# Two layers of attention and MLP, forward and backward: w2's products of layer 1 spread over its backward pass, and the last turns of w1 set behind the first products

## The chip, the cores and the metric

The kernel runs on one core of one Trainium2 chip. Its time is the device time of one execution in microseconds (us); the median of three runs of the kernel before is 1107.51 us (1107.36 to 1107.98). A core has TensorE (PE; its weight loads are shown apart as PEld), VectorE (DVE), ScalarE (ACT), GpSimd (POOL) and SyncE (SP), which run their own instruction lists and wait for one another by semaphores, and 16 DMA engines that move data between the chip's memory (DRAM) and the on-chip memory SBUF. PE writes into the banks of PSUM.

## What is computed

Two layers, each an attention block that reads a cache and an MLP, for two sequences of one token, and then the gradients of everything against a given `grad_out`:

```python
def _A_ref(x, k_cache, v_cache, wq, wo):      # Hq = 32, Hkv = 4, Sk = 16384, Dh = 128
    q = (x @ wq).reshape(B, Sq, Hq, Dh).transpose(0, 2, 1, 3)
    k = jnp.repeat(k_cache, rep, axis=1)
    v = jnp.repeat(v_cache, rep, axis=1)
    p = _softmax(jnp.einsum("bhqd,bhkd->bhqk", q, k) * (Dh ** -0.5))
    o = jnp.einsum("bhqk,bhkd->bhqd", p, v)
    return o.transpose(0, 2, 1, 3).reshape(B, Sq, Hq * Dh) @ wo

def _B_ref(x, w1, b1, w2, b2):                # D = 1024, F = 3584
    h = _gelu(jnp.einsum("bsd,df->bsf", _layernorm(x), w1) + b1)
    return jnp.einsum("bsf,fd->bsd", h, w2) + b2

x = A_x
x = x + _A_ref(_layernorm(x), k_cache, v_cache, wq, wo)
x = x + _B_ref(_layernorm(x), w1, b1, w2, b2)
x = x + _A_ref(_layernorm(x), k_cache, v_cache, wq, wo)
x = x + _B_ref(_layernorm(x), w1, b1, w2, b2)
```

`out_0` is x at the end; `out_1` to `out_9` are the gradients of x, of the K and V caches, and of the weights and biases. Both layers share the caches and the weights, so each of the four passes (forward of layers 0 and 1, backward of layers 1 and 0) reads the caches and the attention weights, and each MLP, forward and back, the MLP weights. The page counts 348.15 MB read and 98.62 MB written. Everything is bfloat16 in DRAM.

## The kernel before

**A list of pieces, planned before it is written out.** The function does not issue instructions as it goes. `emit(fn, uses)` appends a piece of work and the memory chunks that it uses to a list, and `Program.run` goes through the list at the end, calls each piece, and so writes the instructions of all engines in the order of the list. Within an engine this is the order of execution.

**Chunks and slots.** A chunk is up to 1 MB of a cache or a weight (`ld_kv`, `ld_rows`, `ld_w2`, ...), or a place without a load (a turned copy, a row to store). A slot is 128 partitions x 4096 bf16, 1 MB. There are 16 slots of their own, and parts of other tiles serve as slots while those tiles are not in use; their names (`ds`, `e`, `late`) stand in the profile. Before layer 0's backward pass some slots end as places of loads and become staging for stores (`HALF_AT`, `FULL_AT`); nine serve loads to the end, one of which the chunk `Y` keeps. `run` asks, ahead of every piece, whether the next load can have a free slot, where next means in the order of the pieces that first use the chunks. It gives the slot if all chunks in between still find room (`possible`), and writes the load's `dma_start` to SP's queue at that place. A chunk gives its slot back after its last piece. SP's queue is in order: a load whose slot is still read, or still being stored from, holds up the loads behind it. `keep` leaves a chunk in its slot between two passes where there is room all the way, so that its second load falls away.

**The backward pass of attention**, `attn_bwd`, runs in steps, `s = 0, 1, ...`. In layer 1's pass, step s turns a piece of a V chunk on DVE (`kblock`, L537) and multiplies it on PE two blocks later (L550); 14 steps behind it (`LAG_B`) a piece of a K chunk is multiplied (`direct`, L575). A V chunk and a K chunk last four steps each. wo's and wq's tiles are turned by PE and ACT (`turn_here`, L452 and L455) and multiplied (`here_products`, L465) in the steps between. There are 128 steps of V and 14 more. The caller hands in `extra`, a table from a step to pieces that are put at that step's end; at the end of the pass they come in the same order.

**What layer 1's `extra` holds.** `w2_fwd_piece(1, ws2b, i, fps1)` is the MLP's second product in the forward direction for w2's tile i of seven: 32 matmuls (L877) into `fps1`. After the seventh, `x_out` adds bias and residual (L1441), and `col_to_row` makes the row of `out_0` of it: two transposes on PE (L616), a copy on DVE (L617) into a chunk of kind `"load"`, that is into a slot of loads, and a store on POOL's queue (L618). The same seven tiles are used once more: each of their 28 pieces is turned in place (`w2_turns`, L452 and L455), and the turned ones are multiplied with layer 0's gradient after the pass (L1526 to L1530), so every tile keeps its slot from its first product to the end.

**The joint between the passes** (L1520 to L1599). After layer 1's pass come its layer norm, w2's products, `dh0_` (L1532, with `spread_h0`, L506 and L507), and the products of w1: `t1` holds sixteen turns on DVE (L437), two for each of eight chunks of w1, and `p1` eight groups of 28 matmuls (L487), one for each chunk. Between the groups stand the first units of w1's and w2's gradients: rows turned and copied (L1289, L1309, L268), outer products (L1326) cast by ACT (L276) and stored by POOL (L1356). Then the layer norm's backward and layer 0's attention pass follow, whose outputs fill PE, DVE and ACT.

Of the kernel before, what the change touches and what calls it, by code (L numbers as in the profile page):

```python
# [57 lines left out]
class Program:  # L58
# [12 lines left out]
    def emit(self, fn, uses=()):  # L71
        i = len(self.ops)
        self.ops.append((fn, tuple(uses)))
        for c in uses:
            if c.first is None:
                c.first = i
            c.last = i
# [105 lines left out]
def kernel(  # L183
# [46 lines left out]
    emit = P.emit  # L230
# [23 lines left out]
    def ob():  # L254
        st["ob"] += 1
        return obanks[st["ob"] % len(obanks)]


    def load_of(engine, us):
        st[engine] += us  # L260
        m = min(st["act"], st["dve"])
        st["act"] = min(st["act"] - m, 6.0)
        st["dve"] = min(st["dve"] - m, 6.0)
# [127 lines left out]
    def ld_w2():  # L391
        return [ld_rows("w2", B_w2, 4 * i, 4, 0, D) for i in range(FJ // 4)]

    def col(c, j, n, o):
        return c.ap[:, j * n + o * 128:j * n + (o + 1) * 128]
# [213 lines left out]
    def col_to_row(colT, dram_out, queue=None, kind="half"):  # L609
        c = P.chunk(kind=kind)  # L610

        def f():
            row = c.ap[0:DJ, 0:256].rearrange("p (b n) -> p b n", b=2)
            ps = ob()[0:DJ, 0:256].rearrange("p (b n) -> p b n", b=2)
            for b in range(2):
                PE.transpose(ps[:, b, :], colT[:, :, b], identf[:])  # L616
            V.tensor_copy(out=row, in_=ps)  # L617
            (queue or GP).dma_start(dram_out.rearrange("b (j n) -> j b n", n=128), row)  # L618

        return f, [c]  # L620
# [252 lines left out]
    def w2_fwd_piece(l, ws, i, fps):  # L873
        def f():
            for j in range(4):
                for o in range(DJ):
                    PE.matmul(fps[:, o, :], lhsT=col(ws[i], j, 1024, o), rhs=h_all[:, 4 * i + j, 2 * l:2 * l + 2],  # L877
                              start=False, stop=True, skip_group_check=True)
        return f, [ws[i]]
# [404 lines left out]
    def y_rows(colT, j0, jn, q, at_):  # L1284

        def f():
            tp = ob().bitcast(BF16)[32 * q:32 * q + 4, 0:jn * 128].rearrange("p (a b) -> p a b", b=128)
            for j in range(jn):
                PE.transpose(tp[:, j, :], colT[:, j0 + j, :], ident[:])  # L1289
            S.copy(out=Y.ap[32 * q:32 * q + 4, at_:at_ + jn * 128], in_=flat(tp))  # L1290
            load_of("act", 0.7)

        return f, [Y]
# [109 lines left out]
    def mark(name):  # L1403
        def f(n=0):
            marks[name, n] = len(P.ops)
        return f
# [11 lines left out]
    def at_sb0(c0, n):  # L1418
        return sb[0][:, c0:c0 + n]
# [20 lines left out]
    def x_out(xn, xT, fps):  # L1440
        V.tensor_tensor(out=xn[:], in0=fps, in1=b2T[:].to_broadcast([128, DJ, 2]), op=ALU.add)  # L1441
        V.tensor_tensor(out=xn[:], in0=xn[:], in1=xT[:], op=ALU.add)
# [21 lines left out]
    xA1 = attn_fwd(1, down, lambda: xM0, mark("e1"), w1_turns[0:2], tw[5][1] + tw[6][0] + tw[6][1] + [(dh_last_, ())])  # L1464
# [29 lines left out]
    xM1 = vec.tile([128, DJ, 2], F32, name="xM1")  # L1494
    fps1 = at_sb0(288, 16).rearrange("p (j b) -> p j b", b=2)
    ws2b = ld_w2()
    extra = {2: [(lambda: V.memset(fps1, 0.0), ())]}
    for i in range(7):
        extra.setdefault(4 + 3 * i, []).append(w2_fwd_piece(1, ws2b, i, fps1))
    extra[26] = [(lambda: x_out(xM1, xA1, fps1), ())]  # L1500

    ws2c = ws2b
    dhps0 = at_sb0(160, 56).rearrange("p (j b) -> p j b", b=2)
    w2_turns = [turn_here(ws2c[j // 4], (j % 4) * 1024, 8) for j in range(FJ)]
    for n, b in enumerate(w2_turns):
        extra.setdefault(28 + 3 * n, []).append(b)

    ws1c = [ld_rows("w1q", B_w1, 4 * h, 4, cg * 896, 896) for h in range(2) for cg in range(4)]
    dm_0 = quads(at_sb0(224, 16))
# [1 line left out]
    t1, p1 = [], []  # L1511
# [3 lines left out]
        p1 += turned_products(lambda n=n: dm_0[:, n // 4], t, 14 * (n % 4), 14, vh0, n % 4 == 0, n % 4 == 3)  # L1515
    for n, b in enumerate(t1[0:2]):
        extra.setdefault(135 + 2 * n, []).append(b)
    extra[30] = [col_to_row(xM1, out_0.rearrange("b s d -> (b s) d"), kind="load")]
    attn_bwd(1, up, lambda: saved["g3"], (None, wo_prods), mark=mark("d1"), extra=extra)
    wo_prods0 = wo_first_ops(0, down[0] % HKV, saved["wo"])[2]  # L1520

# [16 lines left out]
    mark("late")()  # L1538
    mark(-1)()
    emit(lambda: S.copy(out=Y.ap.bitcast(I32), in_=wide["n"][:, 0:2].bitcast(I32).to_broadcast([128, CH // 2])), [Y])  # L1540
    for b in t1[9:]:
        emit(*b)
    emit(lambda: load_of("dve", 6.0))
    first = [y_rows(gM_all, 0, 8, 0, 0)] + dw_units("h", 0, 0, pieces_rows(out_8, F, D))
    rest_h = first[15:]
    for n, b in enumerate(p1):
        emit(*b)
        for u in first[n + (n > 0):n + 2]:
            emit(*u)
    va0, spread_a0 = spread(lambda: gA_all[:, :, 0:2], DJ, "va")  # L1550
    g1p = mlp_in_bwd(0, lambda dm: unquad(dm[:].rearrange("p (c j) b -> p c j b", j=4), dm_0), g2, parts=True)
# [5 lines left out]
    extra = {4: [(spread_a0, ())]}  # L1557
# [91 lines left out]
```

## Time and profile before

| | |
|---|---|
| median of three runs | 1107.51 us |
| the profiled execution | 1108.07 us |
| its span, first to last instruction | 1106.3 us |
| mean granted clock of TensorE | 0.726 of full speed |
| busy in the span: PE, DVE, ACT, POOL | 73%, 69%, 45%, 16% |
| DMA | 448.98 MB, mean 406 GB/s |

The profile is one execution, and its times count from the span's start. A page cuts the span into 40 equal slices and gives in tenths how busy each engine and the DMA engines were. A row of a table by stage has the stretch, its length, then busy time and number of instructions of PE, PEld, DVE, ACT and POOL (or of those of one line alone), the clock granted to TensorE, the mean busy share of the 16 DMA engines, and the GB/s that they moved. A row of waits reads "who <- for whom: us in total, times, longest". A row of the timeline has start, length, engine, line, operation, what is written from what is read, how many instructions are merged in it, and in brackets the idle time before it and what ended it. A group of instructions has its count, busy time and mean nanoseconds of one, and the idle time before them. A row of DMA issues has their number, the KB of each, and the median time from issue to landing. SPq and POOLq are the queues from which SP and POOL issue DMAs.

### The profile page before, as it was taken

Reading aid. Unit: us, or ns where it says so; the run is one execution under the profiler, and the core shown is the slowest. Engines: PE = TensorE matmul, PEld = TensorE weight load, DVE = VectorE, ACT = ScalarE, POOL = GpSimd, SP = SyncE. Lnnn points to the kernel's source line nnn. Section 1 sums busy time; section 2 is a strip of 40 time slices with the busy share of each in tenths; the row PEclk is TensorE's granted clock in tenths of the full one; section 3 lists DMA queues with packets and bytes.
Section 4 is the critical chain, followed back from the end, with each engine's and each line's share of the span. In section 5 each row is a group of like instructions: output and inputs, shape, how many; then the busy total and the mean of one; then the engine's idle time right before and its main releaser. Section 6 shows DMA issues by size and latency. Waiting matters only on the chain. (4 is left out here: it accounts for less than half of the span.)

```text
span 1106.3 us, 34160 instructions
## 1 busy us (share of the span) xinstructions
PE 808.9 (73%) x14665; PEld 608.4 (55%) x14677; DVE 760.4 (69%) x1472; ACT 492.9 (45%) x1133; POOL 181.7 (16%) x575
## 2 busy tenths in 40 slices
PE   5665666457888656788778678878796896598886
PEld 4554565456777556788778564444353443344453
DVE  5864665069888637765746476979786895598984
ACT  0422223102243221135544327767675785477874
POOL 1000000001000000111211102423332332233330
PEclk9755555555555555557978657999998998799998
DMA  9999999999999999999999989999999999999996
GB/s 379 422 422 422 421 424 422 395 402 397 414 422 421 422 421 377 417 369 416 418 422 421 417 322 413 346 402 423 420 414 424 423 419 421 426 395 419 411 423 268
DMA packets 97932, 448.98 MB, mean 406 GB/s; under 512 B 7624, under 2 KB 11742, under 8 KB 59380
## 3 DMA queue, kind: packets, MB, share of 16 engines
q1 hardware_dynamic: 80532, 351.32, 78.1%
q0 software_dynamic: 17248, 95.48, 21.0%
q8 instruction: 115, 1.88, 0.6%
q14 instruction: 37, 0.30, 0.1%
HBM read 348.15 MB, written 98.62 MB: 404 GB/s over the span
## 5 line engine op out<-in xcount | busy, mean ns | idle before, releaser
L537 DVE STREAM_TRANSPOSE kT<-slot 128x512 int32<-128x512 int32 x420 | 283.2, 694 | 107.5 <-PE sc L550 88.3
L550 PE MATMUL sc<-qbd,kT 128*128 128x32 bf16 x4096 | 262.9, 222 | 10.8 <-DVE kT L537 9.8
L550 PEld LDWEIGHTS <-kT 128*128 128x128 bf16 x4096 | 209.5, 116 | 60.8 <-issue 30.3
L575 PEld LDWEIGHTS <-slot 128*128 128x128 bf16 x3520 | 143.9, 103 | 110.5 <-issue 48.8
L575 PE MATMUL sb<-xt,slot 128*128 128x8 bf16 x3520 | 161.2, 176 | 50.8 <-DMA slot<-in_A_v_cache_dram 24.1
L276 ACT CAST slot<-sc 128x512 bf16<-128x512 f32 x281 | 160.8, 593 | 61.3 <-PE sc L1266 25.5
L1266 PE MATMUL sc<-slot,late 128*128 128x512 bf16 x343 | 128.9, 396 | 28.9 <-DVE slot L279 15.8
L279 DVE CAST slot<-sc 128x512 bf16<-128x512 f32 x172 | 115.2, 678 | 28.4 <-PE sc L1266 11.0
L768 ACT ACTIVATE e<-sc 128x512 bf16<-128x512 f32 x32 | 19.0, 597 | 236.4 <-DVE sc L765 168.8
L276 ACT CAST slot<-sb 128x512 bf16<-128x512 f32 x151 | 89.5, 593 | 36.4 <-PE sb L1326 24.9
L455 ACT COPY slot<-tp 128x512 int32<-128x512 int32 x88 | 50.4, 587 | 95.9 <-PE tp L452 81.5
L1266 PEld LDWEIGHTS <-late 128*128 128x128 bf16 x512 | 44.6, 98 | 62.1 <-issue 49.1
L452 PE MATMUL tp<-ident,slot 128*128 128x128 bf16 x768 | 71.6, 255 | 8.4 <-ACT slot L455 4.2
L585 ACT COPY xt<-e 32x128 int32<-32x128 int32 x256 | 75.7, 296 | 3.9
L1266 PE MATMUL sb<-slot,late 128*128 128x512 bf16 x163 | 65.0, 399 | 8.2 <-DVE slot L279 2.4
L437 DVE STREAM_TRANSPOSE slot<-slot 128x1024 int32<-128x1024 int32 (+1 forms) x48 | 55.3, 1178 | 15.5 <-DMA slot<-in_A_wq_dram 5.7
L1326 PE MATMUL sc<-slot,late 128*128 128x512 bf16 x155 | 58.4, 399 | 10.0 <-DVE slot L279 6.1
L452 PEld LDWEIGHTS <-slot 128*128 128x128 bf16 x768 | 58.1, 116 | 10.6 <-issue 5.0
L279 DVE CAST slot<-sb 128x512 bf16<-128x512 f32 x80 | 54.1, 677 | 10.6 <-PE sb L1266 7.2
L645 POOL TENSOR_TENSOR m_rstd<-ln_vpe,neghalf 128x2 f32<-128x2 f32 x2 | 1.4, 719 | 349.7 <-DVE ln_vpe L643 349.7
L585 POOL COPY xt<-late 32x64 int32<-32x64 int32 x240 | 55.6, 232 | 12.8 <-DVE late L1054 1.7
L585 POOL COPY xt<-ds 32x64 int32<-32x64 int32 x128 | 29.7, 232 | 155.1 <-DVE ds L1054 103.6
(298 smaller groups left out, 1100.0 us busy)
## 6 DMA issues: line engine op xcount, KB each, us to landing
slot<-in_A_k_cache_dram SPq DMA_DIRECT2D x105, 1024.0 KB, 15.7
slot<-in_A_v_cache_dram SPq DMA_DIRECT2D x97, 1024.0 KB, 16.5
out_dram<-slot POOLq DMA_DIRECT2D x55, 1024.0 KB, 14.9
slot<-in_A_wq_dram SPq DMA_DIRECT2D x25, 1024.0 KB, 15.8
slot<-in_A_wo_dram SPq DMA_DIRECT2D x25, 1024.0 KB, 16.5
slot<-in_B_w_dram SPq DMA_DIRECT2D x23, 896.0 KB, 16.2
out_dram<-slot POOLq DMA_DIRECT2D x40, 512.0 KB, 15.0
slot<-in_B_w_dram SPq DMA_DIRECT2D x12, 1024.0 KB, 13.6
```

Of the source, the lines that this page charges most:

```text
L276: S.copy(out=dst, in_=src)
L279: V.tensor_copy(out=dst, in_=src)
L437: V.transpose(out=t.ap[:, h * nw * 256:(h + 1) * nw * 256].bitcast(I32).rearrange("p (w j m) -> p w j m", j=4, m=32), in_=c.ap[:, 0:4 * nc ...
L452: PE.transpose(tp[:, j * 128:(j + 1) * 128], c.ap[:, off + j * 128:off + (j + 1) * 128], ident[:])
L455: S.copy(out=d.bitcast(I32), in_=tp.bitcast(I32))
L537: V.transpose(out=kT[:].bitcast(I32).rearrange("p (w j m) -> p w j m", w=4, j=4), in_=c.ap[:, (i % 4) * 1024:(i % 4 + 1) * 1024].bitcast(I ...
L550: PE.matmul(sc[:, a0:a0 + 4, :, 2 * (i % 4) + q], lhsT=kv[:, 2 * q + w, :, e], rhs=qbd[:, q_at(g), 2 * w + e], start=(w == 0 and e == 0), ...
L575: PE.matmul(acc, lhsT=c.ap[:, n * 128:(n + 1) * 128], rhs=xv[:, i // 4, t // 2, :, 2 * (i % 4) + t % 2], start=(fresh and i == 0 and t == ...
L585: (GP.tensor_copy if on[t % len(on)] == "g" else S.copy)(out=d[32 * t:32 * t + 32, c0:c0 + cn, j, :], in_=s[32 * j:32 * j + 32, c0:c0 + cn ...
L768: S.activation(out=e_of(l, g)[:, 8 * f:8 * f + 8].rearrange("p a h b -> p h a b"), in_=sc[f][:].rearrange("p h (a b) -> p h a b", b=8), fu ...
L1266: PE.matmul(ps, lhsT=hold["blk"][:, j, :], rhs=flat(qm(w)[:, hf * 4:hf * 4 + 4, :]), start=True, stop=True)
L1326: PE.matmul(ps, lhsT=hold[j // 4 * 4][:, j % 4, :], rhs=Y.ap[:, y_at + c0:y_at + c0 + cn], start=True, stop=True)
```

## The change

```diff
@@ -1496,14 +1496,14 @@
     ws2b = ld_w2()
     extra = {2: [(lambda: V.memset(fps1, 0.0), ())]}
     for i in range(7):
-        extra.setdefault(4 + 3 * i, []).append(w2_fwd_piece(1, ws2b, i, fps1))
-    extra[26] = [(lambda: x_out(xM1, xA1, fps1), ())]
+        extra.setdefault(26 + 13 * i, []).append(w2_fwd_piece(1, ws2b, i, fps1))
+    extra[106] = [(lambda: x_out(xM1, xA1, fps1), ())]
 
     ws2c = ws2b
     dhps0 = at_sb0(160, 56).rearrange("p (j b) -> p j b", b=2)
     w2_turns = [turn_here(ws2c[j // 4], (j % 4) * 1024, 8) for j in range(FJ)]
     for n, b in enumerate(w2_turns):
-        extra.setdefault(28 + 3 * n, []).append(b)
+        extra.setdefault(29 + 13 * (n // 4) + 3 * (n % 4), []).append(b)
 
@@ -1515,7 +1515,7 @@
     for n, b in enumerate(t1[0:2]):
         extra.setdefault(135 + 2 * n, []).append(b)
-    extra[30] = [col_to_row(xM1, out_0.rearrange("b s d -> (b s) d"), kind="load")]
+    extra[111] = [col_to_row(xM1, out_0.rearrange("b s d -> (b s) d"), kind="load")]
     attn_bwd(1, up, lambda: saved["g3"], (None, wo_prods), mark=mark("d1"), extra=extra)
@@ -1538,14 +1538,12 @@
     mark("late")()
     mark(-1)()
     emit(lambda: S.copy(out=Y.ap.bitcast(I32), in_=wide["n"][:, 0:2].bitcast(I32).to_broadcast([128, CH // 2])), [Y])
-    for b in t1[9:]:
-        emit(*b)
     emit(lambda: load_of("dve", 6.0))
     first = [y_rows(gM_all, 0, 8, 0, 0)] + dw_units("h", 0, 0, pieces_rows(out_8, F, D))
     rest_h = first[15:]
     for n, b in enumerate(p1):
         emit(*b)
-        for u in first[n + (n > 0):n + 2]:
+        for u in first[n + (n > 0):n + 2] + t1[max(9, 8 + 2 * n):10 + 2 * n]:
             emit(*u)
```

In layer 1's backward pass the seven forward pieces of w2 stand at steps 26, 39, ... 104 in place of 4, 7, ... 22. The four turns of tile i stand 3, 6, 9 and 12 steps behind its piece, so the first is at step 29 and the last at 116, in place of 28 to 109. x is made at step 106 in place of 26, and the row of `out_0` at 111 in place of 30. In the joint, the last seven of w1's sixteen turns no longer stand ahead of all eight groups of products: one stands behind the first group and two behind each of the next three, after the units that stand there. Nothing is computed in another way, and no instruction is added or removed.

## The prediction, made before the changed kernel was run

> **What bounds the kernel now.** I read the page first, then a table by stage, since the DMA is full almost everywhere and only the stretches where it is not can give time back. All loads go through SP's one queue, in the order of their first use. "Slot" is one of the 1 MB places in SBUF that loads land in.
>
> ```profile
> span 1106.3 us, 34160 instructions
> ...
> DMA  9999999999999999999999989999999999999996
> ...
> 450.00:465.00 15.00, 12.68 (x320) 12.02 (x320) 12.83 (x23) 1.94 (x8) 1.86 (x8) 0.50 1.04 419
> 465.00:490.00 25.00, 22.21 (x421) 20.63 (x419) 13.14 (x28) 9.14 (x25) 3.76 (x16) 0.50 1.01 419
> 490.00:495.00 5.00, 4.57 (x107) 4.36 (x104) 3.96 (x7) 1.47 (x4) 0.91 (x2) 0.73 0.51 154
> 495.00:638.00 143.00, 107.95 (x2476) 103.46 (x2476) 82.97 (x146) 66.51 (x176) 23.90 (x103) 0.78 1.02 418
> ...
> 655.00:665.00 10.00, 8.31 (x209) 7.02 (x210) 6.66 (x13) 5.39 (x11) 2.20 (x7) 0.50 0.69 262
> 665.00:690.00 25.00, 21.22 (x246) 12.60 (x248) 15.16 (x38) 17.76 (x40) 3.59 (x7) 0.76 1.01 413
> 690.00:730.00 40.00, 35.24 (x406) 18.88 (x405) 36.09 (x57) 31.02 (x58) 14.53 (x44) 1.00 0.97 355
> 730.00:1080.00 350.00, 280.75 (x3366) 151.63 (x3373) 276.54 (x474) 244.39 (x490) 118.22 (x348) 0.93 1.02 418
> ```
>
> The columns are the stretch, its length, busy time of PE, PEld, DVE, ACT and POOL, granted clock, DMA share and GB/s. Layer 1's backward pass is the stretch from 450 to about 638. It moves 418 GB/s, the full rate, but for five microseconds at 490, which move 154. Then comes the joint to layer 0's backward pass (638 to 673) and that pass itself. In layer 1's pass the engines wait for loads, and its last wait is for a load too:
>
> ```profile
> PE sb L575 <- DMA slot<-in_A_k_cache_dram: 8.8, 7, 3.4
> DVE kT L537 <- DMA slot<-in_A_v_cache_dram: 8.0, 5, 3.4
> ...
> PE sb L575 <- DMA slot<-in_A_k_cache_dram: 2.9, 1, 2.9
> ```
>
> The first two are waits of 495 to 638, the third is the one of 638 to 673: the K products of the last step wait for the last K tile, and the whole joint hangs on them. So what the DMA loses inside 450 to 638 is lost for the end: the joint and all that follows start that much later. The five microseconds at 490 lose (418 - 154) / 418 x 5 = **3.2 us**. The waits of SP's queue between 484 and 493.5, and the instructions around it, name the cause:
>
> ```profile
> SPq L373 <- DMA out_dram<-ds: 7.9, 1, 7.9
> ...
> 484.62 0.38 SPq L378 DMA_DIRECT2D slot<-in_A_wq_dram  x1
> 492.94 0.33 SPq L373 DMA_DIRECT2D ds<-in_A_v_cache_dram  x1
> ...
> 489.85 0.61 PE L616 MATMUL sb<-identf,xM 128*8 128x128 f32 x2
> 490.50 0.41 DVE L617 CAST ds<-sb 8x256 bf16<-8x256 f32 x1 [0.59 <-PE sb L616]
> 491.20 0.68 POOL L618 DMA_DIRECT2D out_dram<-ds  x1 [5.73 <-DVE ds L617]
> ```
>
> The row of the output out_0 borrows a load slot (step 30 of the pass), and the next V load is given the same slot. SP reaches that load after 484.62, waits 7.9 us for the borrowed slot's store, and nothing behind it can be issued. Two things make it a hole. The store comes late, and the queue ahead of it had run dry, because seven w2 tiles had been taken in by step 22 and held seven slots, while PE was nearly full (34.9 of 40 us from 450 to 490, at clock 0.50).
>
> **The change, part by part.** *w2's products* (seven pieces of 32 matmuls, L877) go from steps 4, 7, ... 22 to 26, 39, ... 104. Their loads go with them, since loads are ordered by first use; the bytes stay, and so do the tiles that are kept from the forward pass (the limit on those is the stretch of layer 1's MLP, where eight w1 tiles and eight turned copies fill the slots; w2's new places all come after it). The piece's price is in
>
> ```profile
> L877 PE MATMUL sb<-h_all,slot 128*128 128x2 bf16 x224 | 7.2, 166 | 0.0
> ```
>
> 7.2 us of PE leave a stretch in which PE is busy 34.9 of 40 us and go where it is idle 143 - 108 = 35 us. With PE the limit of steps 0 to 30, these steps end up to 7.2 us sooner, slots come free sooner, and the seven loads that step 30 no longer needs are K, V, wo and wq tiles instead. I take it that the DMA does not run dry there: -3.2 us. Bounds: 0, if a hole stays for another reason, and -3.7, with the 401 GB/s of 495 to 505 mended as well ((418 - 401) / 418 x 10 = 0.4):
>
> ```profile
> 495.00:505.00 10.00, 8.26 (x208) 8.06 (x209) 8.46 (x14) 8.02 (x23) 3.48 (x15) 1.00 1.01 401
> ```
>
> *The turns of w2* (28 of eight PE transposes and one ACT copy) go from steps 28 to 109, evenly, to groups of four behind each piece, to step 116. Their number and their engines stay; one costs 0.61 us of PE at full clock, 1.01 at half, and 0.59 of ACT:
>
> ```profile
> 493.32 0.61 PE L452 MATMUL tp<-ident,slot 128*128 128x128 bf16 x8
> ...
> 471.63 1.01 PE L452 MATMUL tp<-ident,slot 128*128 128x128 bf16 x8
> ...
> L455 ACT COPY slot<-tp 128x512 int32<-128x512 int32 x69 | 39.3, 587 | 51.1 <-PE tp L452 50.8
> ```
>
> PE and ACT have 35 and 76 us of idle time in that stretch, so 0; without that cover the four that move past step 109 would cost 4 x 1.0 us.
>
> *out_0's row* goes from step 30 to 111. Its two transposes, its copy and its POOL store are the same; what is queued behind it is again the next load. From the transposes (489.85) to the load that takes the slot (492.94) the trace has 3.1 us; that is what SP will be held up. What decides is how far the queue is ahead then:
>
> ```profile
> slot<-in_A_v_cache_dram SPq DMA_DIRECT2D x14, 1024.0 KB, 13.7
> ...
> 604.82 0.41 SPq L373 DMA_DIRECT2D slot<-in_A_v_cache_dram  x1
> 606.07 0.33 SPq L373 DMA_DIRECT2D slot<-in_A_k_cache_dram  x1
> ```
>
> V loads of 505 to 640 land 13.7 us after their issue, which is five tiles in flight at 2.5 us each (1.049 MB at 418 GB/s). Step 111 is at about 604, where these two are issued (by the order of loads they are for steps 120 and 122). A load issued 3.1 us later still lands in its turn, with 10 us to spare: 0, with 3.2 us, the old hole, as the upper bound. POOL and DVE have no other long wait there: the exchanges of that head lie at steps 107 and 115.
>
> *The products p1 ahead of the remaining turns of w1* (seven DVE transposes, five chunks' worth of program order). In the trace these are on different engines and neither waited:
>
> ```profile
> 652.06 1.09 DVE L507 TENSOR_TENSOR kT<-sc,quad 128x896 bf16<-128x896 f32 x1 [0.44 <-PE sc L506]
> 653.07 7.52 DVE L437 STREAM_TRANSPOSE slot<-slot 128x896 int32<-128x896 int32 x7
> ...
> 653.20 0.89 PE L487 MATMUL sb<-kT,slot 128*128 128x8 bf16 x28 [1.18 <-DVE kT L507]
> 655.37 0.94 PE L487 MATMUL sb<-kT,slot 128*128 128x8 bf16 x28
> ...
> 662.71 0.94 PE L487 MATMUL sb<-kT,slot 128*128 128x8 bf16 x28
> 663.51 0.59 PE L1326 MATMUL sc<-slot,late 128*128 128x512 bf16 x1
> ```
>
> The first product starts 0.05 us after its own operand, while the turns run, and DVE has nothing else between 653 and 663. DVE's and PE's own orders therefore stay as they are. What moves is memory: the turned copies of chunks 5 to 7 are asked for after the first products have freed theirs, so the V loads can have their slots sooner. Today they wait for the last turn:
>
> ```profile
> 650.56 0.82 SPq L373 DMA_DIRECT2D slot<-in_A_v_cache_dram  x2
> ...
> 660.61 0.80 SPq L373 DMA_DIRECT2D slot<-in_A_v_cache_dram  x2
> ...
> 671.21 0.33 SPq L373 DMA_DIRECT2D slot<-in_A_k_cache_dram  x1
> 690.40 0.38 SPq L378 DMA_DIRECT2D slot<-in_A_wo_dram  x1
> 700.27 0.33 SPq L373 DMA_DIRECT2D slot<-in_A_v_cache_dram  x1
> ```
>
> The last turn ends at 660.59, the loads go out at 660.61. They could go at about 654, and the hole of 655 to 665, (418 - 262) / 418 x 10 = 3.7 us, would close. But layer 0's pass then runs on slots: SP issues no load between 671.21 and 690.40 and the DMA loses (418 - 355) / 418 x 40 = 6.0 us more from 690 to 730, where PE, DVE and ACT are the limit (35, 36 and 31 of 40). By 730 the loads that were issued are those already used plus the eight permanent slots, whenever the first of them came. A load that comes 6 us sooner lengthens the later gap: 0. Against it, the turned copy of chunk 5 may get the slot of chunk 1, whose product ends at 656.3, and the turns end 1.1 us later, at 661.7; p1's last product (662.71) needs them. Bounds -3.7 and +1.1; I take +0.2, near the row 662.71, which leaves a microsecond.
>
> **Sum.** -3.2 + 0 + 0 + 0.2 = -3.0: a span of 1103.3 us. The profiled run took 1108.07 us around its span of 1106.3, and the median is 1107.51, so 1107.5 - 3.0 = **1104.5 us**.
>
> **The rivals.** (a) *The hole only moves.* The store at step 111 dries the queue as it did at 490: 1104.5 + 3.2 = 1107.7. For it: slots are scarcer there, with all seven w2 tiles in. Against it: 13.7 us of lead. (b) *The joint pays too.* The 3.7 us of 655 to 665 are kept, because after 730 the DMA is the limit again (418 GB/s): 1100.8. Against it: the 19 us without a load after 671. (c) *Slower: the end of layer 1's pass runs short of slots.* From step 104 to 126 (about 593 to 626) seven w2 tiles, two of wo, two of wq and out_0's row leave five of seventeen slots for K and V, and the last w2 tile has come only now. The nearest row for a stretch short of slots is layer 1's MLP:
>
> ```profile
> 430.00:445.00 15.00, 9.08 (x246) 8.66 (x246) 10.58 (x30) 2.14 (x7) 0.94 (x5) 0.50 0.91 344
> ```
>
> At its 344 GB/s, 33 us lose (418 - 344) / 418 x 33 = 5.8 us: 1104.5 + 5.8 = 1110.3. It decides from a loss of 3.0 us on, a mean of 380 GB/s there. Against it: w2 holds as many slots there today, at full rate. (d) *Slower: PE stays at half clock.* Scaled from 0.78 to 0.50, 107.95 us become 168, with w2's pieces 175, against 143 us plus the time of some six w2 loads (15) for the DMA: 17 us over, 1121. Against it: a PE that is behind is a full PE, and after the full 465 to 490 the clock rose, 0.50, 0.73, 0.78 in the table.
>
> The Trainium skill, "TensorE: Matmul & The Clock Gate", Part 1, has a rule of this kind: the throttled state is the default, and some 3.4 us of sustained activity release it. By that rule a thinner PE load in steps 0 to 30 would put the release off, which is (d); the trace agrees with the release after a full stretch and cannot show what a thinner one would do.
>
> **How the numbers follow.** Forecast 0.58 (own range 1103 to 1106), (a) 0.12, (b) 0.12, (c) 0.13, (d) 0.05. A measurement of this kernel can tell about 0.2%, 2.2 us, from no change. Faster than 1105.3: 0.47 of the forecast's 0.58 and (b), 0.59; the same: 0.11 and (a), 0.23; slower: 0.18. The range from (b)'s 1100.8 to 1109.5 leaves out (d) and most of (c).
>
> **What would show it.** Right: no row of SP waiting for an out_dram store at step 30, 490 to 495 at full rate, the last K tile about 3 us sooner, reads still 348 MB; the V loads of the joint out before 656, and the gap after 671 as long as that gain. Wrong: the rate under 400 GB/s near step 111; a PE clock of 0.50 through the pass; or 690 to 730 fuller than 355 GB/s, which would be (b).

## The result, and the profile after

The changed kernel takes 1106.15 us (median of 22 runs), the kernel before 1107.94 us (22 runs on the same chip): a ratio of 0.9981, with a 95% interval of 0.9974 to 0.9987, or 2.1 us saved (1.4 to 2.9). The forecast was 1104.5, or 3.0 saved. The profiled execution has a span of 1102.9 us against 1106.3.

The table by stage of the changed kernel, columns as before:

```profile
490.00:495.00 5.00, 4.02 (x103) 3.80 (x101) 4.46 (x8) 3.68 (x12) 1.85 (x8) 1.00 1.00 410
495.00:638.00 143.00, 111.44 (x2660) 106.53 (x2657) 80.38 (x145) 63.62 (x167) 22.98 (x97) 0.80 1.01 413
...
655.00:665.00 10.00, 7.59 (x179) 6.09 (x180) 6.78 (x17) 4.84 (x12) 2.23 (x7) 0.50 1.01 420
665.00:690.00 25.00, 21.57 (x255) 12.63 (x255) 16.52 (x38) 18.26 (x39) 5.13 (x11) 0.77 0.80 297
690.00:730.00 40.00, 35.50 (x405) 18.89 (x405) 35.48 (x55) 31.42 (x58) 12.97 (x39) 1.00 0.97 367
```

The hole at 490 is gone: 410 GB/s instead of 154. The joint's hole at 655 is gone too (420 for 262), but the stretch behind it has a new one of the same kind (297 for 413). And the long stretch of layer 1's pass moves 413 where it moved 418: something is lost inside it. To see where, I count in DMA time. In a stretch of full transfer this kernel moves 420 GB/s, so a stretch loses (420 - rate) / 420 of its length. First the kernel before, then the changed one:

```profile
0.00:460.00 460.00, 297.27 (x6756) 265.98 (x6757) 298.40 (x655) 103.51 (x311) 10.78 (x42) 0.55 1.01 411
460.00:500.00 40.00, 35.73 (x767) 33.75 (x765) 25.07 (x48) 14.73 (x41) 6.92 (x28) 0.59 0.95 387
600.00:620.00 20.00, 13.78 (x323) 13.15 (x321) 10.94 (x18) 6.53 (x20) 1.86 (x8) 0.67 1.02 418
620.00:740.00 120.00, 93.76 (x1576) 63.51 (x1576) 86.45 (x162) 70.56 (x147) 30.11 (x96) 0.79 0.97 374
460.00:740.00 280.00, 222.31 (x4454) 186.47 (x4454) 180.94 (x333) 140.79 (x331) 55.59 (x204) 0.76 0.99 395
740.00:1060.00 320.00, 256.41 (x3027) 136.41 (x3034) 252.05 (x426) 220.74 (x437) 104.29 (x296) 0.93 1.02 418
```

```profile
0.00:460.00 460.00, 297.40 (x6666) 264.81 (x6667) 298.54 (x656) 103.90 (x312) 11.33 (x44) 1.00 1.01 412
460.00:500.00 40.00, 35.34 (x756) 33.46 (x756) 26.25 (x48) 15.98 (x42) 6.80 (x30) 0.91 1.03 417
600.00:620.00 20.00, 15.33 (x344) 14.77 (x340) 12.30 (x21) 6.98 (x17) 3.46 (x13) 0.74 0.94 378
620.00:740.00 120.00, 92.54 (x1539) 62.27 (x1543) 84.54 (x162) 69.23 (x145) 29.29 (x92) 0.78 0.96 375
460.00:740.00 280.00, 223.88 (x4545) 187.68 (x4548) 181.16 (x337) 140.13 (x329) 55.13 (x202) 0.81 0.99 397
740.00:1060.00 320.00, 259.60 (x3056) 137.68 (x3063) 253.94 (x426) 223.69 (x441) 104.90 (x296) 0.92 1.02 420
```

From 460 to 740, where the change has its pieces, the loss falls from 16.7 us (25 / 420 x 280) to 15.3, by 1.3 us. At 490 the gain is 3.1 - 0.3 = 2.8; a new loss of 2.0 us stands between 600 and 620. The other stretches differ between executions of the kernel before itself; a second profile of it has

```profile
0.00:460.00 460.00, 295.73 (x6740) 264.43 (x6740) 296.32 (x653) 101.92 (x304) 9.51 (x36) 0.79 1.01 410
...
740.00:1060.00 320.00, 257.58 (x3030) 137.04 (x3037) 253.09 (x431) 221.09 (x440) 105.28 (x302) 0.92 1.02 420
```

410 in the first and 420 in the last. So of the 3.4 us by which the two spans differ, about 1.3 are the change's by this count, just under what was measured (the rate is rounded to 1 GB/s, which is 0.7 us).

The new loss is at the row of `out_0`. In the changed kernel SP's queue waits there from 600 to 612 (us in total, times, longest):

```profile
SPq L373 <- DMA out_dram<-slot: 7.3, 1, 7.3
```

The timeline of SP, PE and POOL around it:

```profile
601.84 0.38 SPq L378 DMA_DIRECT2D slot<-in_A_wq_dram  x1
609.61 0.33 SPq L373 DMA_DIRECT2D slot<-in_A_v_cache_dram  x1
...
602.59 0.38 PE L616 MATMUL sc<-identf,xM 128*8 128x128 f32 x2
603.77 0.68 POOL L618 DMA_DIRECT2D out_dram<-slot  x1 [8.85 <-DVE slot L617]
```

And the store's time from issue to landing, in the changed kernel:

```profile
out_dram<-slot POOLq DMA_DIRECT2D x1, 4.0 KB, 5.7
```

and in the kernel before:

```profile
out_dram<-ds POOLq DMA_DIRECT2D x1, 4.0 KB, 1.7
```

From the transposes to the next load it is 7.0 us now, 3.1 before. The store of 4 KB is issued 1.2 us behind the transposes (1.35 before), but it takes 5.7 us to land beside full DMA engines, and took 1.7 when the queue had run dry and they moved little.

The chain from the start of layer 1's pass through the joint, first before, then after. Its first row is a copy in the layer norm's backward just ahead of the pass, its last row the same copy behind the products of w1; the joint starts at the last K products (L575):

```profile
441.98 0.17 DVE L517 COPY uq<-sb 128x16 f32<-128x16 f32 x1 [1.00 <-PE sb L487]
...
638.37 1.02 PE L575 MATMUL sb<-xt,slot 128*128 128x8 bf16 x32 [2.86 <-DMA slot<-in_A_k_cache_dram]
...
644.42 6.15 PE L465 MATMUL sb<-gM_all,slot 128*128 128x2 bf16 x224 [1.51 <-DVE gM_all L1194]
651.68 0.34 PE L506 MATMUL sc<-dh_all,selp 128*128 128x56 bf16 x4 [1.11 <-DVE dh_all L1533]
...
663.69 0.18 DVE L517 COPY uq<-sb 128x16 f32<-128x16 f32 x1 [3.10 <-PE sb L487]
```

```profile
441.95 0.17 DVE L517 COPY uq<-sb 128x16 f32<-128x16 f32 x1 [1.00 <-PE sb L487]
...
635.43 1.03 PE L575 MATMUL sb<-xt,slot 128*128 128x8 bf16 x32 [3.45 <-DMA slot<-in_A_k_cache_dram]
...
641.49 5.98 PE L465 MATMUL sb<-gM_all,slot 128*128 128x2 bf16 x219 [1.51 <-DVE gM_all L1194]
649.15 0.27 PE L465 MATMUL sb<-gM_all,slot 128*128 128x2 bf16 x5 [1.68 <-issue]
649.73 0.34 PE L506 MATMUL sc<-dh_all,selp 128*128 128x56 bf16 x4 [0.31 <-DVE dh_all L1533]
...
661.74 0.17 DVE L517 COPY uq<-sb 128x16 f32<-128x16 f32 x1 [1.49 <-PE sb L487]
```

The last K products come 2.9 us sooner, as forecast. But between the 219th and the last five of w2's products with layer 0's gradient PE stands still for 1.68 us and waits for nothing that the profile shows. The spread of that gradient (L506) is 14.3 us behind the last K products instead of 13.3: 1.0 us of the 2.9 is lost again (of the stall's other 0.7 most had been L506's wait for DVE, 1.11 us before and 0.31 now). From L506 to the last row it is 12.0 us in both. So the whole stretch, from the first row to the last, falls from 221.7 to 219.8 us: 1.9 us, near the 2.1 measured. (The expectations below count this stretch to the first weight load of L506: 12.0 us before, 13.8 after.)

### The profile page after: what moved, and what is told of

The parts are those of the page before. It is cut to its first block, busy times and chain, and to the rows that moved or that the text cites. A ratio compares the mean times of both kernels' runs of the same rounds, so it can differ in the third digit from the quotient of the medians.

```text
span 1102.9 us, 34164 instructions
## 1 busy us (share of the span) xinstructions
PE 809.1 (73%) x14665; PEld 607.6 (55%) x14677; DVE 759.6 (69%) x1472; ACT 492.6 (45%) x1133; POOL 181.7 (16%) x575
## 3 DMA queue, kind: packets, MB, share of 16 engines
q8 instruction: 115, 1.88, 0.6%
## 5 line engine op out<-in xcount | busy, mean ns | idle before, releaser
L537 DVE STREAM_TRANSPOSE kT<-slot 128x512 int32<-128x512 int32 x436 | 294.1, 695 | 109.5 <-PE sc L550 90.9
L575 PEld LDWEIGHTS <-slot 128*128 128x128 bf16 x3456 | 141.9, 103 | 101.4 <-issue 45.3
L575 PE MATMUL sb<-xt,slot 128*128 128x8 bf16 x3456 | 157.6, 177 | 45.7 <-DMA slot<-in_A_v_cache_dram 23.9
L452 PE MATMUL tp<-ident,slot 128*128 128x128 bf16 x768 | 74.4, 260 | 11.0 <-DMA slot<-in_A_wq_dram 5.7
L1326 PE MATMUL sc<-slot,late 128*128 128x512 bf16 x155 | 58.7, 401 | 13.8 <-DVE slot L279 9.9
L437 DVE STREAM_TRANSPOSE slot<-slot 128x1024 int32<-128x1024 int32 (+1 forms) x46 | 52.9, 1178 | 18.6 <-DMA slot<-in_A_wo_dram 9.1
## 6 DMA issues: line engine op xcount, KB each, us to landing
out_dram<-slot POOLq DMA_DIRECT2D x55, 1024.0 KB, 14.3
```

The source lines that it names most:

```text
L437: V.transpose(out=t.ap[:, h * nw * 256:(h + 1) * nw * 256].bitcast(I32).rearrange("p (w j m) -> p w j m", j=4, m=32), in_=c.ap[:, 0:4 * nc ...
L452: PE.transpose(tp[:, j * 128:(j + 1) * 128], c.ap[:, off + j * 128:off + (j + 1) * 128], ident[:])
L537: V.transpose(out=kT[:].bitcast(I32).rearrange("p (w j m) -> p w j m", w=4, j=4), in_=c.ap[:, (i % 4) * 1024:(i % 4 + 1) * 1024].bitcast(I ...
L575: PE.matmul(acc, lhsT=c.ap[:, n * 128:(n + 1) * 128], rhs=xv[:, i // 4, t // 2, :, 2 * (i % 4) + t % 2], start=(fresh and i == 0 and t == ...
L1326: PE.matmul(ps, lhsT=hold[j // 4 * 4][:, j % 4, :], rhs=Y.ap[:, y_at + c0:y_at + c0 + cn], start=True, stop=True)
```

## The experiments

All ratios are against the kernel before, on the same chip. "Loss" is the DMA time lost from 460 to 740, from the rate of that one stretch; rounded as above. "Pass" is the time from the first row of the chain above to the last K products, "to L506" from there to the spread of layer 0's gradient, each from the kernel's one profile; from L506 to the chain's last row it is 12.0 us in all, 12.1 with 32 pairs more. "Stall" is PE's, among w2's products in the joint.

| kernel | ratio, 95% interval | loss, us | pass, us | to L506, us | stall, us |
|---|---|---|---|---|---|
| before | 1 | 16.7 | 196.4 | 13.3 | none |
| before, again | 1.0003 [0.9994, 1.0011] | 16.7 | 196.3 | 13.3 | none |
| turns of w1 only | 1.0002 [0.9994, 1.0011] | 16.7 | 196.5 | 13.3 | none |
| the whole change | 0.9981 [0.9974, 0.9987] | 15.3 | 193.5 | 14.3 | 1.7 |
| w2 spread, row at 111 | 0.9984 [0.9974, 0.9994] | 15.3 | 193.4 | 14.3 | 1.7 |
| the same, row in its own place | 0.9981 [0.9973, 0.9990] | 15.3 | 193.5 | 14.3 | 1.7 |
| the change, row in its own place | 0.9978 [0.9968, 0.9988] | 15.3 | 193.3 | 14.4 | 1.8 |
| the change, one w1 load later | 0.9986 [0.9977, 0.9995] | 15.3 | 193.3 | 14.3 | 1.7 |
| the change, 32 pairs more | 0.9988 [0.9979, 0.9996] | 16.0 | 194.1 | 14.4 | 1.8 |
| the change, 96 pairs more | 0.9988 [0.9977, 0.9999] | 15.3 | 194.4 | 13.2 | none |
| row at 111 only | 0.9979 [0.9970, 0.9988] | 14.0 | 193.3 | 13.3 | none |
| row in its own place only | 0.9960 [0.9947, 0.9972] | 14.0 | 193.6 | 13.3 | none |
| row in its own place, and turns | 0.9968 [0.9957, 0.9980] | 14.0 | 193.4 | 13.3 | none |
| change, own place, w1 loads later | 0.9974 [0.9965, 0.9984] | 13.3 | 193.1 | 13.1 | none |

The two columns of the chain split the kernels cleanly: without the hole at 490 the pass is 2.8 to 3.3 us shorter (2.0 and 2.3 with the added pairs), and each stall costs 1.0 us behind it. The ratios agree with this, but most of their intervals are too wide to tell 1 us.

**The change in halves.** First the spread of w2 with the row at 111 and the turns of w1 as before, then the turns alone (the last hunk of the change):

```diff
-        extra.setdefault(4 + 3 * i, []).append(w2_fwd_piece(1, ws2b, i, fps1))
-    extra[26] = [(lambda: x_out(xM1, xA1, fps1), ())]
+        extra.setdefault(26 + 13 * i, []).append(w2_fwd_piece(1, ws2b, i, fps1))
+    extra[106] = [(lambda: x_out(xM1, xA1, fps1), ())]
...
-    extra[30] = [col_to_row(xM1, out_0.rearrange("b s d -> (b s) d"), kind="load")]
+    extra[111] = [col_to_row(xM1, out_0.rearrange("b s d -> (b s) d"), kind="load")]
```

> w2's products and turns and the row of out_0 moved as in the change, w1's turns left ahead of the products. Theory (the gain is the closed hole of 490 to 495, less a new hole near 607; the turns give nothing): 1 to 3 us under before, ratio 0.997 to 0.999, the same as the full change within 1 us; a row of SP waiting some 7 us for an out_dram store near 605 and 2 us lost there; the V loads of the joint go out only at the end of the last turn, near 658. Rival (the turns carry the gain): ratio 1.000.

> Only w1's last turns set behind the first products; w2 as before. Theory: no gain, ratio 0.999 to 1.001: the hole of 490 to 495 stays at about 150 GB/s, the hole of 655 to 665 closes and the one after 671 grows by as much. Should PE's stall of 1.7 us among w2's products in the joint come from the loads that now run beside it, it shows here too and the ratio is up to 1.0015. Rival (the closed hole of the joint pays): 3.7 us less, ratio 0.9967.

The spread with the row at 111: 0.9984, the whole gain. The turns alone: 1.0002; the joint, 620 to 740, loses what it lost before,

```profile
620.00:740.00 120.00, 95.99 (x1604) 65.64 (x1604) 86.11 (x155) 69.46 (x143) 27.52 (x86) 0.78 0.96 375
```

375 GB/s against 374. Loads that go out sooner in the joint bring nothing: from L506 to the end of the chain above it is 12.0 us with either order.

**The row in a place of its own.** The row goes into a small tile instead of a load slot, so that no load waits for its store: at step 30 with everything else as before, at step 111 with the whole change, and at step 111 with the spread alone.

```diff
-        c = P.chunk(kind=kind)
+        c = None if kind == "own" else P.chunk(kind=kind)
...
-            row = c.ap[0:DJ, 0:256].rearrange("p (b n) -> p b n", b=2)
+            row = small.tile([16, 2, 128], BF16, name="r16", bufs=1)[0:DJ] if c is None else c.ap[0:DJ, 0:256].rearrange(
+                "p (b n) -> p b n", b=2)
...
-        return f, [c]
+        return f, [] if c is None else [c]
```

> The kernel before, but the row of out_0 at step 30 is copied into a small tile of its own and no load waits for its store. Theory (the store's wait for a load slot makes the hole at 490): the row of SP waiting for out_dram is gone, 490 to 495 moves 330 GB/s or more, 2 to 3 us less, ratio 0.997 to 0.998. Rival (the slots were used up anyway, since the seven w2 tiles came early and PE was behind): the hole stays near 150 to 250 GB/s and the ratio is 0.999 to 1.000.

> The full change, with the row of out_0 at step 111 in a small tile of its own. Theory (the change's new hole near 607 is the store's, which holds a load slot for 7 us): 600 to 620 back at 418 GB/s, and 1.5 to 2.5 us less than the change, ratio to before 0.995 to 0.997. Rival (slots are short there with all seven w2 tiles in): the rate near 607 stays under 390 GB/s and the time is the change's, 0.998.

> The change's spread of w2 and the row at step 111, the turns as before, the row in a small tile of its own. Theory that the spread is neutral: no DMA time lost at 490 nor at 607, and the ratio is 0.995 to 0.997, that of the row in its own place without the spread. Rival that the spread costs about 2 us somewhere behind step 104 (short of slots, or a wait in the joint): ratio 0.9972 to 0.9985, and 620 to 740 loses 1 to 2 us more of DMA time than the 13 us of the kernel before.

At step 30, with w2 as early as before, the hole is gone and the ratio is 0.9960, below the expected 0.997 to 0.998. Its stages, 460 to 500 and the sum:

```profile
460.00:500.00 40.00, 34.95 (x763) 32.97 (x761) 24.40 (x47) 15.08 (x40) 6.25 (x25) 0.62 1.02 414
...
460.00:740.00 280.00, 220.53 (x4445) 183.86 (x4447) 182.09 (x338) 141.02 (x331) 54.80 (x202) 0.77 1.00 399
```

So the borrowed slot alone made the hole; the seven early w2 tiles did not. The stages account for 2.7 us and the pass for 2.8, the ratio for 4.4 (3.1 to 5.9, from five runs); what the rest is stays open. But the change with its row in a place of its own is no better than the change (0.9978), against what I expected. Nor is the spread with its own place for the row (0.9981), as its rival had it:

```profile
600.00:620.00 20.00, 14.15 (x346) 13.40 (x345) 11.29 (x20) 8.21 (x19) 2.52 (x9) 0.83 1.02 417
620.00:740.00 120.00, 93.91 (x1550) 63.75 (x1553) 85.65 (x160) 69.18 (x145) 29.57 (x94) 0.77 0.96 368
460.00:740.00 280.00, 226.07 (x4562) 189.89 (x4565) 182.36 (x335) 141.66 (x336) 55.86 (x206) 0.77 0.99 397
```

The hole at 607 is gone (417 GB/s), and 620 to 740 loses 14.9 us instead of 13.1 (374 GB/s with the row in a load slot): the sum stays at 397. Two things follow. The store at 111 cost nothing in the end. And the spread costs some 1.3 us of DMA time that a kernel without it does not pay, wherever the DMA shows them.

**The row alone, the own place with the turns, and the kernel before once more.** The first moves only the row, from step 30 to 111 in a load slot; the second is the row's own place at step 30 with the turns' hunk; the third has no edit.

```diff
-    extra[30] = [col_to_row(xM1, out_0.rearrange("b s d -> (b s) d"), kind="load")]
+    extra[111] = [col_to_row(xM1, out_0.rearrange("b s d -> (b s) d"), kind="load")]
```

> The kernel before, with out_0's row at step 111 instead of 30, still in a load slot; w2's products early, as before, the turns as before. Theory now (the only thing that made the hole at 490 was the borrowed slot, and w2's products are of no account): 490 to 495 moves over 400 GB/s, a hole of about 2 us of DMA time appears between 600 and 620, behind a wait of SP of about 7 us for an out_dram store, and the ratio is 0.997 to 0.9995, as with the whole change and the spread alone. Rival (the prediction's second reason: the seven early w2 tiles had run the queue dry and PE was full): without the spread a loss of 1 us or more stays between 465 and 500, and the ratio is 0.9995 to 1.001.

> The kernel before with the row in a place of its own at step 30, and the change's order of products and turns in the joint. Theory that the turns give nothing: ratio 0.995 to 0.997, and 620 to 740 loses 13 us of DMA time as before, only at other places. Rival (the joint's hole pays once the one ahead of it is gone): 0.992 to 0.994, with 10 us lost from 620 to 740.

> The kernel before, unchanged, for a second profile of it: which of its losses are its own and which are of one execution. Theory: ratio 1.000; the loss of 3.2 us at 490 and the 13 us of 620 to 740 are there again within 0.5 us; the loss of 2 us between 940 and 1060, which the kernel before and one experiment showed and four others did not (0.5 to 1.5), differs by up to 1.5 us from execution to execution. Rival: it is 2 us again, and part of what the change gained there is the change's own.

The row alone closes the hole at 490 and has 0.9979, what the whole change has; its loss at 607 is smaller than expected, 0.8 us:

```profile
460.00:500.00 40.00, 34.91 (x753) 32.78 (x751) 25.62 (x49) 15.28 (x45) 7.42 (x32) 0.58 1.02 417
600.00:620.00 20.00, 13.87 (x317) 13.17 (x312) 10.85 (x20) 6.45 (x18) 2.52 (x9) 0.66 1.00 403
...
460.00:740.00 280.00, 222.77 (x4484) 187.35 (x4484) 183.39 (x338) 142.15 (x337) 56.58 (x209) 0.76 0.99 399
```

With the turns added to the own place the ratio is 0.9968, inside what was expected for it and not to be told from 0.9960. The kernel before again: 16.7 us lost from 460 to 740, as the first time, and nothing from 740 to 1060, where its first profile had lost 1.5.

**What stops PE among w2's products.** Up to here the stall of 1.7 us among w2's products is in all kernels with the spread and in none without. The page counts the packets that bring instructions, and PE's matmuls and weight loads:

```profile
PE 809.1 (73%) x14665; PEld 607.6 (55%) x14677; DVE 759.6 (69%) x1472; ACT 492.6 (45%) x1133; POOL 181.7 (16%) x575
...
q8 instruction: 115, 1.88, 0.6%
```

115 packets of 16 KB (1.88 MB / 115) for 29,342 instructions of PE are 255 for each: PE's program comes in blocks of 256 instructions, or 128 matmuls with their weight loads. In w2's products PE takes 27 ns for such a pair, and so a block in 3.5 us. If one border of blocks is behind the 219th product, the one ahead of it is behind the 91st. Two experiments move the border: they do the eight transposes of four, or twelve, of w2's turns twice, which adds 32 or 96 such pairs ahead of the joint. A third leaves the program and sends one w1 load later.

```diff
-            for j in range(n):
+            for j in list(range(n)) * (2 if twice else 1):
                 PE.transpose(tp[:, j * 128:(j + 1) * 128], c.ap[:, off + j * 128:off + (j + 1) * 128], ident[:])
...
+    w2_turns = [turn_here(ws2c[j // 4], (j % 4) * 1024, 8, twice=j < 4) for j in range(FJ)]
```

The third (`behind` makes the planner give that load only the slot that the named chunk had):

```diff
+    ws1c[6].behind = ws2c[0]
```

> The whole change, with the eight transposes of w2's first four turns done twice: 32 matmuls and 32 weight loads more on PE in layer 1's pass, where it has idle time. Theory (the stall is where PE's program crosses from one 16 KB block of instructions, 256 of 64 bytes, to the next): the stall moves 32 products forward, to 187 of 224, and stays near 1.7 us. Rival (a semaphore or a unit of work that the profile doesn't show, tied to the data): it stays after 219. Ratio as the change's, 0.997 to 0.999.

> The same with twelve turns done twice: 96 matmuls and 96 weight loads more. Theory: the blocks' borders move by 96 products, from 91 and 219 to 5 products before the first and 123 behind it; the first border is then crossed ahead of the 1.5 us in which PE waits, the next block is asked for some 3 us earlier in PE's own time, and the stall falls under 0.4 us; from the last K products to the spread of layer 0's gradient 12.0 to 12.3 us, ratio 0.9965 to 0.998. Rival (as above): the stall stays at 219 and at 1.7 us; or it stands at 123 with 1.7 us, if what is late isn't the asking but the way.

> The whole change, but the seventh of the eight w1 loads of the joint is tied to the slot of w2's first tile, so that it goes out some 7.8 us after the last K products instead of 2.4, and the eighth at about 9.5, as before the change. The change showed a stall of PE of 1.7 us after 219 of the 224 products of w2 with layer 0's gradient, as in all four kernels with the spread and in none of the six without. PE's next 16 KB of instructions came 5.4 us after the first of these products, against 3.1 to 3.5 without the stall. Theory (the fetch of instructions stands behind data packets, and the early w1 load keeps the DMA engines full there): the stall is gone or under 0.4 us, the fetch comes at 3 to 4 us, and from the last K products to the turned copies of w1's first product it is 12.0 to 12.3 us instead of 13.9. Rival (the stall is tied to the spread in another way, such as the late turns of w2's tiles): it stays at 1.7 us, and the stretch at 13.8 to 14.0 us. Ratio 0.9965 to 0.9978 or 0.9975 to 0.9988.

With 32 more the stall moved 32 products forward, to the 187th:

```profile
642.49 5.12 PE L465 MATMUL sb<-gM_all,slot 128*128 128x2 bf16 x187 [1.51 <-DVE gM_all L1194]
649.38 1.13 PE L465 MATMUL sb<-gM_all,slot 128*128 128x2 bf16 x37 [1.77 <-issue]
```

With 96 more it is gone:

```profile
643.82 6.11 PE L465 MATMUL sb<-gM_all,slot 128*128 128x2 bf16 x224 [1.50 <-DVE gM_all L1194]
```

So the stall is PE waiting for its next block of instructions. The traces show it in another way too. Counted over all of PE's records from the start (29,387 in the changed kernel: the matmuls, the weight loads and 45 of its sequencer), all 38 idle times of PE of more than 1 us that the fourteen profiles put down to "issue", that is, to no wait that they show, stand at the same place of a block of 256, 193 or 194 records behind a multiple of it. They are not the spread's alone: most lie inside layer 1's pass, where PE has time to spare, and the kernel before has one there:

```profile
512.67 0.20 PE L575 MATMUL sb<-xt,late 128*128 128x8 bf16 x2 [1.13 <-issue]
```

Among w2's products no such time is spare. (Both ratios are 0.9988, so neither kernel is better than the change; for 96 more 0.9965 to 0.998 was expected. Without the stall L506 comes 13.2 us behind the last K products instead of 14.3, but the pass, which holds the added transposes, is 0.9 us longer than the change's, and the loss is 15.3 us all the same.) The load sent later changed nothing: 0.9986, and the stall stayed at 1.67 us after 219. The load went out 7.0 us behind the last K products, near the 7.8 that was meant, but the DMA engines were full all the same:

```profile
600.00:620.00 20.00, 14.73 (x362) 14.05 (x361) 11.16 (x19) 8.49 (x23) 2.52 (x9) 0.78 0.94 381
640.00:650.00 10.00, 7.82 (x274) 7.67 (x272) 7.37 (x17) 0.00 (x0) 0.52 (x1) 0.50 1.06 404
```

So that run did not test what it was meant to. That the bytes not moved at 607 (381 GB/s from 600 to 620) filled the engines at 640 is likely, but not shown.

The last run changes both: the row in its own place, so no hole at 607, and two w1 loads later.

```diff
+    ws1c[6].behind, ws1c[7].behind = ws2c[1], ws2c[3]
```

> The whole change with the row of out_0 in a place of its own, so that no store holds the queue, and the seventh and eighth w1 load of the joint tied to the slots of w2's second and fourth tile, so that they go out 7.8 and 9.5 us after the last K products, as before the change. PE crosses into the block whose fetch was late 8.5 us after the last K products; the kernel before moved about 250 GB/s there, the change 400. Theory (the fetch is late because it stands behind data in DMA engines that are full): at that point the rate is under 320 GB/s, the fetch starts within 1.2 us of the crossing, the stall of 1.7 us is gone (under 0.4), from the last K products to the spread of layer 0's gradient it is 12.0 to 12.3 us, and the DMA loses 13.5 to 14.0 us from 460 to 740, as with the row in its own place without the spread; ratio 0.9955 to 0.9972. Rival (the late fetch belongs to the spread in another way): the stall stays at 1.7 us after 219 products, the loss is 15 us or more, ratio 0.9972 to 0.9985.

Its stages at w2's products and from 460 to 740, and the row of the products in the timeline (L467 is L465 of the others):

```profile
640.00:650.00 10.00, 7.58 (x259) 7.37 (x257) 8.16 (x18) 0.14 (x1) 0.52 (x1) 0.50 0.93 333
...
460.00:740.00 280.00, 222.11 (x4566) 186.01 (x4569) 183.25 (x340) 142.00 (x337) 56.56 (x209) 0.80 1.00 400
```

```profile
643.65 6.11 PE L467 MATMUL sb<-gM_all,slot 128*128 128x2 bf16 x224 [1.51 <-DVE gM_all L1197]
```

The stall is gone with the spread in place and the program's borders where they were, and the loss is 13.3 us, the least of all. The ratio is 0.9974, a little above the expected 0.9972, its interval on both sides of it: the rate, the stall and the loss came as the theory had them, but the time alone does not tell it from the rival, nor from the same kernel with its w1 loads early (0.9978), against which the chain to L506 is 1.5 us shorter. The kernels that close the hole and have no stall lie at 0.9960 to 0.9979 (0.9988 with 96 pairs more), and their intervals overlap; the simplest of them, the row in its own place, has the lowest ratio, from five runs.

The trace's record of each instruction packet gives the same in all fourteen profiles. "Crossed" is PE's passing of the border ahead, "fetch" the start of the next packet's transfer, and the rate is that of the DMA between the two:

```
                                   crossed   fetch   later by   GB/s   stall
before                              646.85  647.58     0.7       248   none
before, again                       648.45  649.37     0.9       263   none
turns of w1 only                    649.79  650.81     1.0       252   none
row at 111 only                     646.01  647.10     1.1       265   none
row in its own place only           643.31  643.99     0.7       256   none
row in its own place, and turns     643.86  644.90     1.0       264   none
change, own place, w1 loads later   646.08  647.11     1.0       242   none
the whole change                    643.92  646.86     2.9       410   1.7
w2 spread, row at 111               644.60  647.52     2.9       411   1.7
the same, row in its own place      645.87  648.83     3.0       405   1.7
the change, row in its own place    644.95  648.11     3.2       377   1.8
the change, one w1 load later       646.87  649.86     3.0       403   1.7
the change, 32 pairs more           644.06  647.06     3.0       407   1.8
the change, 96 pairs more           647.10  650.24     3.1       406   none
```

Seven profiles with the DMA at 242 to 265 GB/s have the packet on its way within 1.1 us; seven at 377 or more need 2.9 to 3.2; in one of these, with 96 pairs more, the next border lies behind w2's products. The rates go with the kernels: all with a low rate but one are without the spread. That one, the change with its own place and w1 loads later, has the spread and the low rate, and no stall; this tells the full DMA engines from the spread itself.

## Why the prediction was right, and where not

The forecast was 1104.5 us, 3.0 under before, and 2.1 (1.4 to 2.9) were saved. By the prediction's own marks this is less than it bet on: 1106.15 lies just outside the forecast's own 1103 to 1106, and above 1105.3, so in what it called the same (0.23), not in faster (0.59). The mechanism of the gain was in the main right; one price was missing.

*The hole at 490.* Right in place and in the first of its two causes, the store that held the slot: 3.2 us were forecast, 2.8 gained by the DMA's rate, 2.9 in the pass. (The term's lower bound, -3.7, is -3.6 by its own figures, 3.2 + 0.4.) The second cause was wrong. I wrote that the queue "had run dry, because seven w2 tiles had been taken in by step 22", and put the gain down to w2's products leaving a full PE. With w2 as early as before and only the row moved, the hole is gone as well, and the ratio, 0.9979, is the whole change's. So the size of this term came out right partly by luck: it was booked to w2's products, and the row's move, booked at 0, brought it. (The row needs all seven products, so there is no kernel with w2 spread and the row left at step 30.) Nor did PE's load fall when they went: in 450 to 490 it was busy 34.9 us before, 34.2 in the changed kernel and 34.5 with the spread alone.

*The turns of w2* were costed at nothing; nothing in the runs speaks against it. *The turns of w1 in the joint*: +0.2 forecast, 1.0002 [0.9994, 1.0011] measured, 0.0 in the chain behind L506, and the joint as a whole moves 375 GB/s with them and 374 without: what the hole at 655 gives, the gap behind 665 takes, as argued. Rival (b), where the joint pays, is refuted.

*The row at step 111*: "A load issued 3.1 us later still lands in its turn, with 10 us to spare: 0". The 0 holds, but the way to it failed. SP was held 7.0 us, the store's 5.7 us beside full engines being the term that I took from a row where it had empty ones, and the DMA lost 2.0 us there. The sum from 460 to 740 is the same with that hole as without it. Rival (a) saw the hole come, but not that it would cost nothing: the pass is 193.5 us with it and 193.3 with the row in its own place. In both kernels the last K load itself waits for a slot that PE's K products (L575) still read, 3.5 and 3.9 us, and goes out 181.9 and 182.5 us into the pass; so it is that slot, and not SP's lost time, that sets it. Why PE gives the slot back no sooner without the hole is not settled.

*The step that failed* is the first: "7.2 us of PE leave a stretch in which PE is busy 34.9 of 40 us and go where it is idle". It gave the move of w2's products no price. It has one, in the joint: with the spread the DMA engines are full while PE runs through w2's products there, its next block of instructions comes 2 us late, and PE's stall takes 1.0 us from the chain. With 1.0 us instead of 0 the sum is -3.0 + 1.0 = -2.0, inside the measured 1.4 to 2.9; the chain itself has -2.9 + 1.0 + 0 = -1.9. (The 1.3 us of DMA time is the same price counted by rate, and less sure: the kernel with 96 pairs more has it without the stall.) Why the DMA engines are that full there with the spread was not tested step by step; sending two of w1's loads later was enough to end it.

Rivals (c) and (d) did not come. Behind step 111 the rate is 413 (620 to 640), and PE's clock in 495 to 638 was 0.80. Rival (d) had come from the rule of the Trainium skill, "TensorE: Matmul & The Clock Gate", Part 1, that the throttled clock is the default and activity releases it. These runs do not test it on a thinner load, since PE was as busy ahead of 490 as before; in the kernel with the spread alone, with w2's products already gone from there, the clock was at full speed by 490:

```profile
490.00:495.00 5.00, 4.03 (x107) 3.82 (x104) 4.72 (x8) 3.14 (x11) 1.84 (x8) 1.00 1.00 412
```

## What to carry to other kernels

A small store out of a slot that a load waits for is priced by the load on the DMA engines when it is issued, not by its size: give it a place of its own. Here that edit alone is better than the whole change (0.9960 [0.9947, 0.9972] against 0.9981 [0.9974, 0.9987]). Where loads come sooner, look at the next burst of short PE instructions on the critical chain: one that runs through a block of 256 in 3.5 us can wait for its own program when the DMA is full.

## What the runs showed of the hardware

- PE's program arrives in DMA packets of 16 KB. In w2's products a packet is under way 0.7 to 1.1 us after PE crosses the border ahead when the DMA moves 242 to 265 GB/s, and 2.9 to 3.2 us after at 377 to 411; at 27 ns for a weight load and its matmul the difference is a stall of 1.7 us. The Trainium skill, "Runtime: NRT & Kernel Launch", section "Instruction fetch mechanics", says that programs are fetched in 16 KiB blocks of 256 instructions while the one before runs, mostly hidden. The block size agrees with the traces (255 for each packet, and 38 stalls at one place of 256); hidden it is not where the DMA is full and PE uses up a block in 3.5 us.
- The store of 4 KB landed after 1.7 us in the three profiles that store it when the queue has run dry, after 3.7 and 4.1 in the two with the row's own place at step 30, and after 4.7 to 5.8 in the nine that store it at step 111 beside full DMA engines.
- In the first 460 us TensorE was granted a mean clock of 0.55 in one execution and 1.00 in another (the 0 to 460 rows above), at 411 and 412 GB/s: in that stretch, where loads set the pace, the clock is not in the time.
